# Four edits to one attention kernel's schedule: where head outputs are placed, when right operands are due, which masks TensorE adds, and how outputs reach x

## The chip, the cores and the metric

The kernel runs on one core of a Trainium2 chip. The metric is the device time of one execution, in microseconds; less is better. A core has TensorE (PE, matrix products, with weight loads shown as PEld), VectorE (DVE), ScalarE (ACT), GpSimd (POOL), and SyncE (SP), which here issues nearly all transfers between DRAM and on-chip memory. Each engine takes its instructions in the order in which the kernel was written down; an instruction that waits holds up everything behind it on its engine.

## The reference, cut

```python
batch, n_heads, seq, head_dim = 4, 8, 768, 64          # block = 32, 24 blocks
scores = (1/sqrt(64)) * q @ k.transpose(0, 1, 3, 2)
scores = where(mask, scores, -1e9)      # window, first/last rows and columns, 3 random blocks a row
attn = exp(scores - max); attn = attn / (attn.sum(-1) + 1e-09)
x = (attn @ v).transpose(0, 2, 1, 3).reshape(B, S, 512)
mixed = real(fft(fft(x, axis=1), axis=2))
u = x + mixed
un = (u - mean(u)) / sqrt(var(u) + 1e-06)              # over the 512 features
out = u + maximum(un @ w_ch1, 0) @ w_ch2               # 512 -> 2048 -> 512
```

## The kernel before

The kernel has two kinds of work: attention, which makes x, and the mixer (Fourier transform, normalizing, channel products), which makes the output from x. They overlap: while batch b is in attention, the mixer of batch b-1 runs beside it, and the mixer of the last batch ends the kernel.

**Attention** goes through 16 pairs n (4 batches with 4 pairs of heads each; batch b has pairs 4b to 4b+3). A pair has 12 units: two halves of the queries ("first" and "second", 384 each) by six key chunks of 128. Two units make a slot, so a pair has six slots. For a unit, TensorE computes scores s (`scores`, L578). The mask is applied in one of two ways. "By TensorE": four more short products (L588) per slot add a large negative number to the scores, and ScalarE's exponential (L598) writes e directly. Or by VectorE: the exponential (L606) stays in TensorE's accumulator, and a multiplication with a mask of 0 and 1 (L608) writes e. The first way is used for batch 0 and then as long as `masks["by_pe"]` is true; it also leaves an addition of e into `acc` per unit (L633 on VectorE or L638 on GpSimd). A slot's e goes to the product with v one or two slots later (`values`, o, L652).

A finished half of a pair, oT, must become columns of x. `place` does it by three transposes on TensorE (xt, L675) and a copy on ScalarE into x (L676). For the pairs 9, 10, 11, 13, 14 and 15 `place_blocks` (L691) does it by transfers: 16 for each half, each of a 32-row piece with 12 KB. There are two buffers of x for each half, so batch b uses those of batch b-2, and the copy of its first pair must wait until the stores of batch b-2 to the output (`out_dram<-x`, L1157) have landed.

**The mixer** of a batch goes: sums of the softmax turned and inverted (st L746, r L749), x scaled by them (`scale_x`, L761), the Fourier transform and the normalizing (utp transposes L992, un L951), and a turn of the normalized rows through DRAM: `un_blocks` writes `far` (L1011), `un_back` reads it as unT (L1020). `right` (L1052, VectorE) makes the four right operands of the Strassen products from unT. Then the channel products start: a `quad` of seven products (xp, yp, z, L1090, with the additions L1095 on VectorE), then `channels`: y (L1146), added to x by VectorE (L1149).

**What sets the order.** One function, `slot`, writes one slot of attention and what stands between it and the next. Channel steps wait in a list `late` and are dealt out at a pace. Mixer steps before the channels wait in `apart`; a planner (`gap`) puts each in when its own running estimate of each engine's time, `when`, says that the step's inputs are ready. Transposes and placements wait in `short` with an estimated ready time. `BACK` is how long after `un_back` the planner holds the right steps of kind "b" back; each of these steps has an estimated cost. `LEAVES` is how long after TensorE's estimated time a placement that reuses x of batch b-2 becomes ready. In `slot`, such a placement of the first half is queued at slot 5 of the batch's first pair, that of the second half at slot 1 of its second pair:

```python
if reuse:
    until(lambda: (b - 2, 0) in finished)
    at = when["PE"] + LEAVES
```

`begin` queues a batch's mixer, and with it a step `go`, which opens the channels and sets `masks["by_pe"]` to false.

Of the kernel before, what the change touches and what calls it, by code (L numbers as in the profile page):

```python
# [11 lines left out]
FP32 = mybir.dt.float32  # L12
# [10 lines left out]
def _words(ap, n):  # L23

    return bass.DRamTensorHandle(ap.tensor.name, (2 * n,), I32)
# [74 lines left out]
def kernel(  # L100
# [14 lines left out]
    nc = tc.nc  # L115
# [4 lines left out]
    P = 128  # L120
    C = S // P
    BLK = 32
# [7 lines left out]
    T = C // 2  # L130
# [54 lines left out]
    far_p = ctx.enter_context(tc.tile_pool(name="far_p", bufs=1, space=bass.MemoryType.DRAM))  # L185
# [7 lines left out]
    when = {"PE": 0.0, "ACT": 0.0, "DVE": 0.0, "POOL": 0.0}  # L193
    free = {"m": [0.0, 0.0], "t": [0.0]}

    def busy(engine, us, after=0.0):
        when[engine] = max(when[engine], after) + us
        return when[engine]

    def bank(tag):  # L200

        at = free[tag].index(min(free[tag]))
        when["PE"] = max(when["PE"], free[tag][at])
        free[tag][at] = float("inf")
        return tag, at

    def give(which, at):
        free[which[0]][which[1]] = at + HOP
# [91 lines left out]
    def bit(n):  # L300
# [5 lines left out]
                      in_=bass.AP(tensor=_words(sampled_blocks, NB * NR), offset=0,  # L306
                                  ap=[[0, NB], [1, 2 * NB * NR]]))
# [135 lines left out]
    for w, w_sb in ((w_ch1, w1_sb), (w_ch2, w2_sb)):  # L443
        rows, cols = w.shape
# [42 lines left out]
    by_pe, to_gather = set(), deque()  # L487
    masks = {"by_pe": True}

    turned, e_of, acc_of, o_of, sums_of, x_of, sp_of = {}, {}, {}, {}, {}, {}, {}  # L490
# [101 lines left out]
    def weigh(u, s):  # L592
        n, w = divmod(u, UP)
        half, c = divmod(w, C)
        e = ep.tile([P, 2, HS], FP32, tag="e", name="e")
        e_of[u] = e
        if u in by_pe:
            nc.scalar.activation(out=e, in_=s[:, :, 0:HS], func=ACT.Exp, scale=scale)  # L598
            e_at[u] = busy("ACT", 0.8, max(s_at[u], e_free.pop(u - 2 * SLOT, 0.0))) + HOP
            if n >= NP:  # L600
                to_gather.append(u)

            if w >= UP - SLOT:
                gather_to(u)
        else:
            nc.scalar.activation(out=s[:, :, 0:HS], in_=s[:, :, 0:HS], func=ACT.Exp, scale=scale)  # L606
            m = mask[:, c, half * HS:(half + 1) * HS].rearrange("p (o s) -> p o s", o=1)
            nc.vector.tensor_tensor(out=e, in0=s[:, :, 0:HS], in1=m.broadcast_to([P, 2, HS]),  # L608
                                    op=ALU.mult)
            e_at[u] = busy("DVE", 0.97, busy("ACT", 0.8, s_at[u]) + HOP) + HOP  # L610
            gather_to(u)
            if n >= NP:
                gather(u)

    def gather_to(u):
        while to_gather and to_gather[0] <= u:
            gather(to_gather.popleft())
# [49 lines left out]
    def place(n, half):  # L667

        b, j = pairs[n]
        oT = o_of.pop((n, half))  # L670
        if j == 0:
            x_of[b, half] = xp.tile([P, T, DM], FP32, tag=("xA", "xB")[half], name="x")
        xt, at = ps_t.tile([P, 512], FP32, tag="t", name="xt"), bank("t")
        for c in range(T):
            nc.tensor.transpose(xt[:, c * P:(c + 1) * P], oT[:, c * P:(c + 1) * P], ident)  # L675
        nc.scalar.copy(out=x_of[b, half][:, :, j * P:(j + 1) * P],  # L676
                       in_=xt[:, 0:HS].rearrange("p (c f) -> p c f", c=T))
        give(at, busy("ACT", 0.5, busy("PE", 0.45, oT_at[n, half]) + HOP))

    def in_blocks(n):  # L680

        return n > 2 * NP and n % NP > 0

    def place_blocks(n, half):
        b, j = pairs[n]
        oT = o_of.pop((n, half)).rearrange("p (c t d) -> p c t d", t=P // BLK, d=BLK)
        for g in range(P // BLK):
            for t in range(P // BLK):  # L690
                nc.sync.dma_start(  # L691
                    out=x_of[b, half][BLK * t:BLK * t + BLK, :, j * P + BLK * g:j * P + BLK * (g + 1)],
                    in_=oT[BLK * g:BLK * g + BLK, :, t, :])

    def into_sums(key, j, sp):
        if j == 0:
# [281 lines left out]
    def mixer(b, xA, xB):  # L978
# [34 lines left out]
        def un_back():  # L1013

            for half in range(2):
                unT[half] = tr_p.tile([P, ND, T * P], FP32, tag="tr", name="unT")
                of = lines[half].rearrange("m (g j) (k a i) -> a j k (m g) i",
                                           j=BLK, a=P // BLK, i=BLK)
                for a in range(P // BLK):
                    nc.sync.dma_start(  # L1020
                        out=unT[half][BLK * a:BLK * a + BLK].rearrange(
                            "j k (g i) -> j k g i", i=BLK),
                        in_=of[a])
            state["back"] = max(when["PE"], state["ready"]) + BACK[b > 0]

        t, s = {}, {}
        K1, K2 = slice(0, ND // 2), slice(ND // 2, ND)

        def spare_room():
            if s:  # L1030
                return
            rest, n, w = room(5, [P, ND * HS], "t4"), HS * ND // 2, P * ND // 2
            t[4] = rest[:, 0:n].rearrange("p (k n) -> p k n", n=HS)
            for i in (1, 3, 4):
                s[i] = rest[:, n:n + w].rearrange("p (k n) -> p k n", n=P)
                n += w

        def right(j, *tiles):

            spare_room()  # L1040
            if 1 not in t:
                both = room(4, [P, ND, HS], "t12")
                t[1], t[2], t[3] = both[:, K1, :], both[:, K2, :], unT[1][:, K1, :]
            b11, b21 = unT[0][:, K1, :], unT[0][:, K2, :]
            b12, b22 = unT[1][:, K1, :], unT[1][:, K2, :]

            def part(ap):
                return ap.rearrange("p k (t n) -> p k t n", n=P)[:, :, tiles[0]:tiles[-1] + 1, :]

            to, a, c = {1: (t[1], b12, b11), 2: (t[2], b22, t[1]), 3: (b12, b22, b12),  # L1050
                        4: (t[4], b21, t[2])}[j]
            tt(out=part(to), in0=part(a), in1=part(c), op=ALU.subtract)  # L1052
# [225 lines left out]
        if not last:  # L1278
            before = first + [pq[1], ar[0][1], ar[1][1], sp[0][1],
                              pq[2], wh[0][1], ft[0][1], ar[0][2], ar[1][2], sp[0][2],  # L1280
                              pq[0], wh[0][2], ft[0][2], ar[0][0], ar[1][0], sp[0][0],
                              sp[1][1], wh[0][0], ft[0][0], sp[1][2], wh[1][1], ft[1][1],
                              sp[1][0], wh[1][2], ft[1][2], wh[1][0], ft[1][0]]
            after = ([("-", un_back, 0.0, 0.0, 0.0)] + le +
                     [("b", lambda i=i: right(i, 0, 1, 2), 0.0, 0.0, 1.0) for i in (1, 2, 3, 4)])
        rest = []
        for r in range(2 if last else 0):
            rest += [(lambda p=p: quad(p), 7 * PRODUCT) for p in range(4 * r, 4 * r + 4)]
# [2 lines left out]
        for r in range(0 if last else NF // 4):  # L1291
# [9 lines left out]
    MOST, LEAST = 9.6, 2.5  # L1301
    COVER = 100.0
    AHEAD = 2.2
    BACK = 13.0, 12.0
    ALONE = 3.0
    LEAVES = 9.0
    SP = UP // SLOT
    SB = SP * NP
    W_PACE = 1.42
# [1 line left out]
    asked = set()  # L1311
    needed = set()
    state = {"paired": False, "total": None, "w": 0, "got": 0, "owed": 0.0, "ready": 0.0,
             "back": 0.0}

    def channel_step():
        late.popleft()[0]()

    def behind(kind):
# [64 lines left out]
    def begin(b):  # L1384


        before, after, rest = mixer(b, x_of[b, 0], x_of[b, 1])
        any_of = len(late) + len(apart) + 4 * len(rest)
        hold = 2 * T
        apart.extend((*step, any_of) for step in norm_steps(b) + before)  # L1390
        apart.extend((*step, hold) for step in after)

        def go():
            late.extend(rest)
            masks["by_pe"] = False
        apart.append(("-", go, 0.0, 0.0, 0.0, hold))

    def rest():
# [19 lines left out]
    def slot(sl):  # L1418
        phase, r = divmod(sl, SB)
        n, s = divmod(sl, SP)  # L1420
# [26 lines left out]
            keep_mask = mask_step(2 * (sl // 3 - 1) + sl % 3 // 2)  # L1447
        for u, ps in got:
            weigh(u, ps)
        if keep_mask:  # L1450
            keep_mask()
        if BY_VECTOR <= n + 1 < len(pairs):
# [16 lines left out]
        if s >= (5 if reuse else 3) and (n, 0) in oT_at and once(n):  # L1469
            b, j = pairs[n]  # L1470
            at = oT_at[n, 0]
            if reuse:
                until(lambda: (b - 2, 0) in finished)
                at = when["PE"] + LEAVES
            if in_blocks(n):
                place_blocks(n, 0)
            else:
                short.append(("t", at, lambda: place(n, 0)))
# [5 lines left out]
        if sl < B * SB and n % NP == 1 and s == 1:  # L1484
            b = pairs[n - 1][0]
            at = oT_at[n - 1, 1]
            if b >= 2:
                until(lambda: (b - 2, 1) in finished)
                at = when["PE"] + LEAVES
            short.append(("t", at, lambda: place(n - 1, 1)))  # L1490
# [43 lines left out]
        while short and (not more or soon) and (  # L1534
                s in must or len(short) > 1 or phase == 0 or soon or sl == B * SB):
            ready = [i for i in short if max(i[1], min(free[i[0]])) <= when["PE"] + 0.1]
# [149 lines left out]
```

## Time and profile before

| What | Value |
|---|---|
| Median of 3 runs | 1059.56 us (1056.76 to 1062.27) |
| Profiled execution | 1059.17 us; span 1057.5 us |
| Mean granted TensorE clock | 0.993 |
| TensorE busy | 1022.8 us (97%), 4338 products |
| VectorE, ScalarE, GpSimd busy | 675.3, 356.2, 240.2 us |
| Placements by transfer x<-oT | 192 of 12 KB, 585 to 1494 ns to issue, median 597 |
| Right steps L1052, first batch | 237.96 to 244.2 us |

Busy time is time in which an engine executed something. TensorE's idle time is 34.7 us in all: 9.6 us before 226, 10.5 after 942 (mostly the last stores), and the rest in short stretches at the hand-overs from one batch's transform to its channel products and to the next batch's attention. A line of the chain of waits gives start, length, engine, operation and line; a line of the wait list gives the engine, the line that waited, what for, the sum in us, how often, and the longest.

### The profile page before, as it was taken

The numbers are of one execution on the slowest core, as the hardware profiler recorded it, in microseconds if no ns is written. First come the engines' busy times: TensorE is split into PE (matmuls) and PEld (weight loads), VectorE is DVE, ScalarE is ACT, GpSimd is POOL, SyncE is SP. The second block draws the span as 40 slices with busy tenths as digits, with TensorE's granted clock in tenths as the row PEclk, the third lists the DMA queues.
The fourth block names the chain that finished last, engine by engine and source line by source line (L and its number), as shares of the span: only waits on it lengthen the run. The fifth ranks groups of instructions, "written<-read, shape, count | busy, mean of one in ns | idle before, by whom it ended". The sixth has DMA issues, their size and how long they took to land.

```text
span 1057.5 us, 12421 instructions
## 1 busy us (share of the span) xinstructions
PE 1022.8 (97%) x4338; PEld 530.7 (50%) x4338; DVE 675.3 (64%) x1235; ACT 356.2 (34%) x718; POOL 240.2 (23%) x270
## 2 busy tenths in 40 slices
PE   8989999997999999999999999899999999999996
PEld 4434345433465553444444654444444654578585
DVE  5899795968745744564578467565457364674663
ACT  6988755562020111342441212153220211210210
POOL 1000183565000100454553001256520001000000
PEclk9999999999999999999999999999999999999998
DMA  7757422292000124212230003821000001000001
GB/s 210 228 177 227 107 47 46 50 140 36 1 0 21 40 30 76 62 32 50 41 56 1 1 10 93 107 39 27 11 11 6 0 1 38 23 1 1 1 17 46
DMA packets 160385, 55.71 MB, mean 53 GB/s; under 512 B 145708, under 2 KB 151098, under 8 KB 160314
## 3 DMA queue, kind: packets, MB, share of 16 engines
q1 hardware_dynamic: 159062, 54.10, 23.9%
q10 hardware_dynamic: 1220, 0.72, 0.3%
q8 instruction: 36, 0.59, 0.2%
q14 instruction: 35, 0.29, 0.1%
q0 software_dynamic: 32, 0.01, 0.0%
HBM read 41.44 MB, written 11.01 MB: 50 GB/s over the span
## 4 chain that ended last, share of the span: by engine, by line
PE 82%; DVE 8%; ACT 3%; DMA 3%; issue 2%; SPq 1%; ACTq 0%; DVEq 0%
PE y L1146 23%; PE z L1090 15%; PE s L578 10%; PE o L652 9%; PE yp L1090 7%; PE yy L1211 7%; PE xp L1090 4%; PE zp L856 2%; ACT e L598 1%; DMA out_dram<-x 1%; PE sp L719 1%; PE s L588 1%; DVE t L1052 1%; DVE x L926 1%; DVE acc L633 1%
## 5 line engine op out<-in xcount | busy, mean ns | idle before, releaser
L638 POOL TENSOR_TENSOR acc<-acc,e 128x384 f32<-128x384 f32 x162 | 163.6, 1046 | 103.8 <-DVE e L608 84.5
L578 PE MATMUL s<-qT,kT 64*128 64x384 f32 x768 | 155.2, 518 | 13.0 <-DVE e L608 6.5
L652 PE MATMUL o<-e,vr 128*64 128x384 f32 x768 | 142.7, 499 | 0.0
L1146 PE MATMUL y<-w_sb,hB 128*128 128x512 f32 x288 | 129.2, 600 | 0.3 <-DVE x L1149 0.3
L1146 PE MATMUL y<-w_sb,hA 128*128 128x512 f32 x288 | 127.9, 595 | 0.0
L1149 DVE TENSOR_TENSOR x<-y,x 128x512 f32<-128x512 f32 x72 | 49.7, 691 | 119.9 <-PE y L1146 119.8
L608 DVE TENSOR_TENSOR e<-s,mask 128x768 f32<-128x768 f32 x90 | 82.0, 951 | 54.9 <-ACT s L606 47.6
L578 PEld LDWEIGHTS s<-qT,kT 64*128 64x128 f32 x768 | 63.8, 186 | 92.3 <-ACT e L598 25.2
L638 POOL TENSOR_TENSOR acc<-e 128x384 f32<-128x384 f32 x42 | 47.1, 1143 | 254.5 <-ACT e L598 124.6
L606 ACT ACTIVATE s<-s 128x768 f32<-128x768 f32 x90 | 68.4, 792 | 89.4 <-PE s L578 89.1
L1090 PE MATMUL z<-unT,t 128*128 128x384 f32 x256 | 93.1, 486 | 2.0 <-DVE hA L1095 2.0
L598 ACT ACTIVATE e<-s 128x768 f32<-128x768 f32 x102 | 77.7, 811 | 48.5 <-PE s L588 32.0
L1146 PEld LDWEIGHTS y<-w_sb,hB 128*128 128x128 f32 x288 | 53.9, 192 | 67.6 <-issue 65.8
L1146 PEld LDWEIGHTS y<-w_sb,hA 128*128 128x128 f32 x288 | 53.7, 190 | 63.7 <-issue 60.2
L652 PEld LDWEIGHTS o<-e,vr 128*64 128x64 f32 x768 | 48.2, 137 | 71.6 <-issue 68.7
L1095 DVE TENSOR_TENSOR hA<-z,hA 128x384 f32<-128x384 f32 x64 | 35.7, 558 | 69.8 <-PE z L1090 69.6
L1099 ACT ACTIVATE hA<-hA 128x384 f32<-128x384 f32 x64 | 33.5, 523 | 129.3 <-DVE hA L1095 129.3
L1090 PEld LDWEIGHTS z<-unT,t 128*128 128x128 f32 x256 | 48.6, 190 | 36.8 <-DVE hA L1095 3.1
L1099 ACT ACTIVATE hB<-hB 128x384 f32<-128x384 f32 x64 | 33.5, 523 | 86.6 <-DVE hB L1095 86.6
L1110 ACT COPY hA<-xp 128x384 f32<-128x384 f32 x32 | 15.3, 478 | 116.0 <-PE xp L1090 116.0
L1090 PE MATMUL z<-t,w_sb 128*128 128x384 f32 x128 | 46.9, 489 | 5.0 <-DVE e L608 3.4
L1090 PE MATMUL z<-t,t 128*128 128x384 f32 x128 | 47.8, 497 | 0.0
(208 smaller groups left out, 1367.0 us busy)
## 6 DMA issues: line engine op xcount, KB each, us to landing
wraw<-in_moe_w_ch_dram SPq DMA_DIRECT2D x32, 512.0 KB
vr<-in_v_dram SPq DMA_DIRECT2D x30, 192.0 KB
far<-un SPq DMA_DIRECT2D x18, 256.0 KB
unT<-far SPq DMA_DIRECT2D x24, 192.0 KB
qb<-in_q_dram SPq DMA_DIRECT2D x44, 96.0 KB
kb<-in_k_dram SPq DMA_DIRECT2D x44, 96.0 KB
x<-oT SPq DMA_DIRECT2D x192, 12.0 KB
out_dram<-x SPq DMA_DIRECT2D x11, 252.0 KB
```

The costliest lines, as they stand in the source:

```text
L578: nc.tensor.matmul(s[:, i, 0:HS], kT[rows, c * P:(c + 1) * P], qT[rows, queries], start=True, stop=u not in by_pe)
L598: nc.scalar.activation(out=e, in_=s[:, :, 0:HS], func=ACT.Exp, scale=scale)
L606: nc.scalar.activation(out=s[:, :, 0:HS], in_=s[:, :, 0:HS], func=ACT.Exp, scale=scale)
L608: nc.vector.tensor_tensor(out=e, in0=s[:, :, 0:HS], in1=m.broadcast_to([P, 2, HS]), op=ALU.mult)
L638: nc.gpsimd.tensor_add(out=acc[:, i, :], in0=start[:, i, :], in1=e[:, i, :])
L652: nc.tensor.matmul(o[D * i:D * i + D, :], vt[:, i, c, :], e[:, i, :], start=(c == 0), stop=(c == C - 1))
L1090: nc.tensor.matmul(to, a[:, k, :], c[:, k, :], start=(k == 0), stop=(k == ND // 2 - 1))
L1095: tt(out=to, in0=ps, in1=a, op=ALU.add)
L1099: nc.scalar.activation(out=h, in_=h, func=ACT.Relu)
L1146: nc.tensor.matmul(y, hs[0, half][:, l, m * P:(m + 1) * P], w2_sb[:, 4 * r + l, :], start=(l == 0), stop=(l == 3))
L1149: nc.vector.tensor_tensor(out=x[:, m, :], in0=y, in1=x[:, m, :], op=ALU.add)
L1211: nc.tensor.matmul(ps, a[:, k, :], c[k // 2][:, k % 2, :] if isinstance(c, list) else c[:, k, :], start=(k == 0), stop=(k == 3))
```

## The change

Four edits.

1. `place_blocks` writes oT to a DRAM buffer `row` in four transfers, then reads it into x in four; the second four wait for the first. It had 16 transfers within the chip.
2. `BACK` has a value for each batch; 13 and 12 stay for batches 0 and 1, and batch 2 has 15 instead of 12. The estimated cost of a right step in batch 0 goes from 1.0 to 1.7.
3. `masks["by_pe"]` becomes false with the first channel step that is written, not with `go`.
4. A first half that reuses x of batch b-2 is placed in the next slot right after that slot's exponentials are written, instead of waiting in `short`; for the second half `LEAVES` goes from 9 to 13.

```diff
     def place_blocks(n, half):
         b, j = pairs[n]
-        oT = o_of.pop((n, half)).rearrange("p (c t d) -> p c t d", t=P // BLK, d=BLK)
+        rows = far_p.tile([BLK, T, P // BLK, P], FP32, tag=f"oT{half}", name="row", bufs=2)
+        oT = o_of.pop((n, half))
         for g in range(P // BLK):
-            for t in range(P // BLK):
-                nc.sync.dma_start(
-                    out=x_of[b, half][BLK * t:BLK * t + BLK, :, j * P + BLK * g:j * P + BLK * (g + 1)],
-                    in_=oT[BLK * g:BLK * g + BLK, :, t, :])
+            nc.sync.dma_start(
+                out=rows.rearrange("r c t f -> r (c t) f")[:, :, BLK * g:BLK * g + BLK],
+                in_=oT[BLK * g:BLK * g + BLK, :].rearrange("r (ct d) -> r ct d", d=BLK))
+        for t in range(P // BLK):
+            nc.sync.dma_start(
+                out=x_of[b, half][BLK * t:BLK * t + BLK, :, j * P:(j + 1) * P],
+                in_=rows[:, :, t, :])
...
-            state["back"] = max(when["PE"], state["ready"]) + BACK[b > 0]
+            state["back"] = max(when["PE"], state["ready"]) + BACK[b]
...
-                     [("b", lambda i=i: right(i, 0, 1, 2), 0.0, 0.0, 1.0) for i in (1, 2, 3, 4)])
+                     [("b", lambda i=i: right(i, 0, 1, 2), 0.0, 0.0, 1.0 if b else 1.7)
+                      for i in (1, 2, 3, 4)])
...
-    BACK = 13.0, 12.0
+    BACK = 13.0, 12.0, 15.0
...
-    LEAVES = 9.0
+    LEAVES = 13.0
...
     def channel_step():
+        masks["by_pe"] = False
         late.popleft()[0]()
...
         def go():
             late.extend(rest)
-            masks["by_pe"] = False
...
         for u, ps in got:
             weigh(u, ps)
+        if state["place"]:
+            state["place"]()
+            state["place"] = None
...
             if reuse:
                 until(lambda: (b - 2, 0) in finished)
-                at = when["PE"] + LEAVES
-            if in_blocks(n):
+                state["place"] = lambda: place(n, 0)
+            elif in_blocks(n):
                 place_blocks(n, 0)
             else:
                 short.append(("t", at, lambda: place(n, 0)))
```

In the changed program VectorE has as many instructions as before, TensorE 12 more products with their weight loads, ScalarE 3 more and GpSimd 2 fewer instructions in the listing, and SyncE 96 fewer transfers. The order on each engine is the same up to about 235 us of the time before.

More of the change, by code (lines that the diff above doesn't have):

```diff
@@ L1313 @@
     state = {"paired": False, "total": None, "w": 0, "got": 0, "owed": 0.0, "ready": 0.0,
-             "back": 0.0}
+             "back": 0.0, "place": None}
     def channel_step():
+        masks["by_pe"] = False
         late.popleft()[0]()
```

## The prediction

> **What bounds the kernel now.** I read the first and fourth parts of the page, then the table of windows cut at the hand-overs between stages, then TensorE's waits, then the chain inside the bad windows. Page, busy time and chain:
>
> ```profile
> PE 1022.8 (97%) x4338; PEld 530.7 (50%) x4338; DVE 675.3 (64%) x1235; ACT 356.2 (34%) x718; POOL 240.2 (23%) x270
> ...
> PE 82%; DVE 8%; ACT 3%; DMA 3%; issue 2%; SPq 1%; ACTq 0%; DVEq 0%
> ```
>
> TensorE bounds, and no edit here takes work from it. So only its idle time (34.7 us) and the time in which it ran at a lower clock can be won. The windows say where that is (columns: window, length, busy time by engine with counts, PEclk granted, DMA share, GB/s):
>
> ```profile
> 238.00:247.00 9.00, 5.64 (x22) 3.02 (x19) 8.93 (x8) 1.53 (x3) 6.37 (x5) 0.98 0.69 104
> 247.00:260.00 13.00, 11.01 (x40) 4.55 (x38) 11.95 (x20) 4.07 (x7) 2.93 (x4) 0.89 0.00 0
> ...
> 400.00:425.00 25.00, 23.04 (x77) 9.45 (x76) 11.50 (x15) 4.68 (x8) 4.35 (x4) 0.93 0.41 66
> ...
> 655.00:695.00 40.00, 34.71 (x139) 15.56 (x139) 22.43 (x33) 12.09 (x25) 10.79 (x12) 0.96 0.74 109
> ...
> 895.00:942.00 47.00, 45.61 (x151) 26.96 (x150) 31.52 (x62) 12.42 (x24) 0.00 (x0) 1.00 0.06 17
> ```
>
> Idle: 3.36 + 1.99, then 1.96, 5.29 and 1.39 us, all at the hand-overs between batches. Between them TensorE is full (260 to 400 idles 0). TensorE's longest waits name the blockers:
>
> ```profile
> PE s L578 <- DVE e L608: 6.5, 3, 3.7
> ...
> PE z L1090 <- DVE e L608: 3.4, 1, 3.4
> PE z L1090 <- DVE hA L1095: 2.0, 1, 2.0
> PE z L1090 <- DVE t L1052: 1.6, 1, 1.6
> ```
>
> The chain in the window 385 to 440 explains the 1.96:
>
> ```profile
> 407.49 2.79 DMA out_dram<-x
> ...
> 410.51 0.48 ACT x L676
> 410.99 0.71 ACT s L606
> 411.72 0.97 DVE e L608
> 412.73 2.35 PE s L578 x8
> 415.08 4.71 PE y L1146 x8
> ```
>
> The copy that places a first half reuses an x buffer whose last store is still under way. It sits at ScalarE's head, and the next exponential queues behind it. The scores after it cost 2.35 instead of 1.49, eight y 4.71 instead of 3.43. The window 655 to 695 has the same with the second half:
>
> ```profile
> 679.45 7.46 DMA out_dram<-x
> ...
> 687.09 0.48 ACT x L676
> 687.57 0.71 ACT s L606
> 688.36 0.97 DVE e L608
> 689.37 2.50 PE s L578 x8
> ```
>
> **The sum's base.** The profiled execution took 1059.17 us (span 1057.5 and 1.7 around it); the median is 1059.56, so terms are taken from 1059.17. A measurement here tells some 0.5% from no change: faster means below 1054.3, slower above 1064.9.
>
> **Masks on TensorE until channels begin.** Three more slots are masked by L588 (0.33 us a slot, 1.0 in all) in place of multiplies L608 on VectorE (six of 0.95). Each now leaves an addition to VectorE L633 (1.0) or to GpSimd, so VectorE is little lighter. What changes is order: before, the first product (z L1090, 242.60 on) waits behind four right steps (237.96 to 244.2), two mask multiplies (244.27, 1.73), the reciprocal and five scalings L761 (246.40 to 250.82). After, the three slots' scores run while the right steps run, the scalings spread over the slots, and the first seven-product group starts with its operands ready. From 235.8 to 269.5 TensorE took 33.7 us for work that sums to 25.8 by its rows (s 1.49, o 1.44, quad 9.03, two of them, xp and yp 1.29 each, the sums): 5.35 idle, the rest low clock (0.63 granted in 247 to 251). After: 25.8 + 1.0 + a new wait. An exponential that writes e directly needs an e buffer, which GpSimd's additions (four units, done at 243.45) free; my replay of the rows puts that wait at 1.3. Sum 28.1 to 28.3: **−5.4**, ends −3 (GpSimd each time 1 us later, and the clock drop stays) and −6.5 (no wait). The 1.7 for the right steps (rows: 0.95 to 1.75) only shifts where the planner puts them, and is in this term.
>
> **First halves behind the next exponentials, batch 2.** After, the exponentials of the next slot stand before the copy L676 on ScalarE, with four more y ahead of it on TensorE. The copy is wanted at about 412.9; the store lands at 410.3. Behind the copy then waits nothing urgent. Gone: 1.96 idle, 0.86 on s, 1.36 on y: 4.2, and from the whole window (21.4 us for 17.1 of work) **−4.3**; ends −2 (idle gone, clock drop not) and −4.5.
>
> Here a page speaks to the size. The row: after 1.96 us of idle the granted clock was 0.50 for 414 to 416 and 0.69 for 416 to 418. The Trainium skill ("TensorE: Matmul & The Clock Gate", Part 1) has the clock halve after an idle window of about 3.4 us; by it the 1.96 would cost no clock and this term would be −2.0, but the trace disagrees, and the trace decides.
>
> **Batch 3: first half, second half (LEAVES 13), due time of the right steps (15).** Before, from 656.0 to 698.75: 42.7 us for 34.7 of work, so 8.0 lost: waits 1.58 and 3.71, s 2.50, o 2.37 for 1.44, and crumbs. After, all scores come ahead of the first product, so the right steps hold nobody (−1.6). But the second half's copy still needs the stores that land at 686.9. SyncE's order is unchanged: four kb loads took 6.6 us (670.41 to 677) behind the unT reads, then the six stores. The copy now stands behind two more exponentials, and the last two queue behind it. The work TensorE has without these two slots ends near 681.3; the first score it can then run comes at 689.3. That is 8.0 idle and about 2.0 of lower clock (as after the 3.71: 0.57 in 690 to 694), 10.0 lost: **+2.0**, ends +3.3 and −8.0 (the stores land before the copy is reached).
>
> **Outputs in eight transfers.** Twelve halves: 16 SyncE issues x<-oT at 0.597 (9.6 us) become four row<-oT, a wait for these to land, and four x<-row. Bounds of an issue: 0.6 (x<-oT, 12 KB) and 1.28 (unT<-far, 192 KB in 128-byte pieces); of a landing: 2.8 (410.3) and 7.5 (686.9). A half: from 4 × 0.6 + 2.8 + 4 × 0.6 = 7.6 to 4 × 1.28 + 7.5 + 4 × 0.6 = 15.0 instead of 9.6; I take 8, since DMA share here is near 0.1 as at 410. Behind SyncE's new wait queue the next pair's qb and kb loads, which are a pair ahead (kb lands near 458 or 496, used a stage later). The trace has one wait for these placements by others that matters: VectorE's scaling at 800.33 waited 3.10, and TensorE did not feel it. The last flip of an output comes some 9 us earlier (one quad less before it), which covers all up to 15: **0**.
>
> **The last hand-over.** With the placement moved, the channel steps left for 876 to 905 run out earlier: in the new order five utp transposes stand in a row where before each had y between. Replaying the rows: the y after the last product end at +14.2, the chain of utp, normalizing (GpSimd's 1.6 in it) and spreading at about 20.3; idle 3.9 instead of 1.2: **+2.5**, ends 0 and +4.
>
> Sum: −5.4 − 4.3 + 2.0 + 2.5 = −5.2: 1059.17 − 5.2 = **1054.0**.
>
> **Rivals.** (1) *Batch 3's stall goes too.* For it: the stores' own data is ready before SyncE gets to them; against: the SyncE order and the unT backlog are the same. Every microsecond of earlier landing gives one. All of it: −5.4 − 4.3 − 7 + 1.5 = −15.2: 1044. (2) *Slower: the DRAM hop sets the last transform.* At 733.12 to 799.06 SyncE carries 64 placements on end; the scaling at 800.33 follows the last, and behind it is the chain that the last hand-over exposes. If a landing of 128-byte pieces takes over 12 us, a half costs 5 + 12 + 2.4 + 12 = 31 on SyncE and in landing against 12; less the 9 of cover that is +10, and the sum is +5 or worse: 1064 to 1070. Against: DMA share is 0.09 in 695 to 830. A page speaks for it: the Trainium skill ("DMA: Bandwidth & Descriptors", Specifications) wants 512 bytes or more and has smaller writes read and rewritten; no row here shows 128-byte writes to DRAM. (3) *The masks' gain is eaten*: e buffers held by GpSimd stop TensorE for 5 us instead of 1.3, after which it resumes at a low clock: about 1058.5. (4) *Batch 3's copy waits longer*: each microsecond of landing after 687 costs one, with the last two exponentials behind it; from 697.5 the whole is slower than 1064.5: 1065. (5) *It does not do what it says*: that ScalarE still takes the copy first; the new order puts the exponentials ahead, so nothing is given to it.
>
> **Numbers.** Forecast 0.41 (its own range 1049 to 1059, half of it below 1054.3); rival 1: 0.25; 2: 0.11; 3: 0.13; 4: 0.10. Faster 0.20 + 0.25 = 0.45; same 0.21 + 0.13 = 0.34; slower 0.21. The range takes in rival 1 to its near side, and the edge of 2 and 4: 1044 to 1064.
>
> **What would show it.** Right: the 3.4 wait of z on e gone; idle in 400 to 425 near 0 and y at 3.43 for eight; one long wait of s near 681 to 689 with L676 waiting for out_dram; POOL or ScalarE named for a wait near 243; one utp wait of 2 to 4 us before 905. Wrong: no wait near 685 (rival 1), L761 waiting over 10 us for x<-row (2), a low clock after 245 (3).

## The result, and the profile after

The changed kernel took 1056.17 us (median of 20 runs, 1054.27 to 1059.40), the kernel before 1059.47 (20 runs, 1056.71 to 1062.27). The ratio is 0.9976, 95% interval 0.9966 to 0.9985: by it 2.5 us faster, clear of no change, and about half of the forecast 5.2 (the two medians differ by 3.3). The profiled execution took 1054.71 us (span 1052.8). It gained 4.5 on the one profiled before, so the pair of profiles shows more than the ratio; the rest of this document looks for the cause of both differences.

Lines in the changed kernel are shifted: z is L1094 (was L1090), y L1150 (L1146), the right steps L1056 (L1052), the stores L1161 (L1157).

The page of the changed kernel, busy time and the chain by engine:

```profile
PE 1023.6 (97%) x4350; PEld 531.4 (50%) x4350; DVE 672.1 (64%) x1232; ACT 356.4 (34%) x718; POOL 236.1 (22%) x264
...
PE 85%; DVE 5%; ACT 2%; SPq 2%; DMA 2%; issue 2%; POOL 1%; ACTq 0%; DVEq 0%; POOLq 0%
```

TensorE still bounds; VectorE's share of the chain fell from 8% to 5%. The same windows (busy time by engine, granted clock, DMA share, GB/s):

```profile
238.00:247.00 9.00, 7.08 (x42) 2.92 (x37) 8.79 (x7) 3.97 (x6) 5.79 (x4) 1.00 0.50 88
247.00:260.00 13.00, 13.00 (x44) 7.78 (x43) 7.49 (x16) 4.08 (x9) 3.86 (x4) 1.00 0.00 0
...
400.00:425.00 25.00, 25.00 (x90) 11.18 (x89) 12.68 (x17) 5.55 (x10) 5.76 (x6) 1.00 0.37 91
...
655.00:695.00 40.00, 35.02 (x137) 15.08 (x137) 24.83 (x31) 13.51 (x27) 21.40 (x20) 0.91 0.61 93
...
895.00:942.00 47.00, 46.43 (x156) 29.66 (x156) 33.31 (x66) 11.83 (x23) 0.52 (x1) 0.96 0.03 6
```

At the first hand-over (238 to 260) TensorE's idle time fell from 5.35 to 1.92 us and the granted clock is 1.00; 400 to 425 has no idle time left. Batch 3's hand-over is no better: about the same idle time (5.29 before, 4.98 after), at a granted clock of 0.91 instead of 0.96.

The 1.9 us that stay at the first hand-over are a wait of s for an exponential (L598), and the chain shows GpSimd's additions ahead of it:

```profile
238.74 5.06 POOL acc L638 x3
...
243.82 0.82 ACT e L598
...
244.69 0.92 PE s L578 x4
```

TensorE's waits in the changed kernel (sum, count, longest):

```profile
PE s L578 <- ACT e L598: 7.6, 11, 2.1
PE s L578 <- DVE e L608: 5.8, 3, 3.7
...
PE utp L996 <- DVE un L955: 1.3, 3, 0.7
PE utp L996 <- ACT unT L997: 0.7, 1, 0.7
```

The waits of z (3.4, 2.0 and 1.6) are gone. The mask multiply still stops s for 3.7, and utp now waits 2.0 in four pieces, all at the last hand-over. In the timeline of TensorE, batch 3's hand-over is (start, length, operation; idle time before it and what ended it):

```profile
674.01 2.93 PE L578 MATMUL s<-qT,kT 64*128 64x384 f32 x8 [3.67 <-DVE e L608]
676.88 2.83 PE L652 MATMUL o<-e,vr 128*64 128x384 f32 x8
681.01 1.78 PE L578 MATMUL s<-qT,kT 64*128 64x384 f32 x8 [1.31 <-DVE e L608]
```

The first wait isn't the copy's. VectorE's timeline shows whose it is:

```profile
666.90 1.18 DVE L1056 TENSOR_TENSOR t<-unT 128x768 f32<-128x768 f32 x1
668.11 1.64 DVE L1056 TENSOR_TENSOR t<-unT,t 128x768 f32<-128x768 f32 x1
669.67 1.75 DVE L1056 TENSOR_TENSOR unT<-unT 128x768 f32<-128x768 f32 x1
671.35 1.74 DVE L1056 TENSOR_TENSOR t<-unT,t 128x768 f32<-128x768 f32 x1
673.01 1.81 DVE L608 TENSOR_TENSOR e<-s,mask 128x768 f32<-128x768 f32 x2
```

Four right steps stand ahead of a slot's two mask multiplies, and with the slot's exponentials (ScalarE, 667.82 to 669.32) long done, TensorE waits for VectorE. The second wait is the copy's; the chain there:

```profile
671.12 7.42 DMA out_dram<-x
...
679.09 0.81 ACT s L606
...
680.00 0.97 DVE e L608
...
681.01 1.78 PE s L578 x8
```

The copy ends last. Without the first wait the scores and o behind it would run earlier, and the second wait would be longer by as much. So the 3.67 cost no time of their own as long as the copy keeps its place; this is worked out from the order, not run.

**A measure by stretch.** To compare kernels I took every product of TensorE in order, gave it a distance to the next product, one price for each line and shape from the trace before, and summed: that is "work". Elapsed time less work is "lost": idle time, low clock, and wider spacing of products. The level of a column depends on the prices; the differences down a column are what counts. Its growth over the same stretches of work, from each trace:

| us lost | first hand-over | to batch 2 | batch 2 | to batch 3 | batch 3 | to the last | last |
|---|---|---|---|---|---|---|---|
| before | 7.8 | 0.2 | 4.6 | 5.4 | 9.3 | 2.9 | 2.0 |
| changed, profile of 1054.71 | 2.5 | 0.8 | 0.4 | 6.3 | 10.1 | 3.3 | 4.3 |
| e5, changed, 1053.63 | 2.4 | 0.8 | 0.4 | 6.3 | 9.5 | 3.3 | 3.6 |
| e9, changed, 1056.83 | 1.8 | 0.8 | 0.4 | 6.3 | 11.7 | 3.3 | 3.6 |
| e10, changed, 1056.23 | 1.9 | 0.8 | 0.4 | 6.3 | 11.5 | 3.3 | 3.6 |
| e1, masks alone | 1.8 | 0.8 | 0.1 | 5.8 | 9.0 | 2.8 | 2.0 |
| e2, first half alone | 10.9 | 0.5 | 0.7 | 5.7 | 9.6 | 2.8 | 2.0 |
| e3, due times alone | 7.8 | 0.2 | 3.0 | 5.6 | 11.9 | 5.0 | 4.9 |
| e4, blocks alone | 6.9 | 0.2 | 3.0 | 5.4 | 9.1 | 2.8 | 2.0 |
| e6, both due times undone | 1.8 | 0.8 | 0.4 | 6.0 | 8.0 | 2.8 | 2.0 |
| e7, BACK undone | 1.8 | 0.8 | 0.4 | 6.3 | 3.8 | 2.8 | 2.0 |
| e8, second half later | 1.8 | 0.8 | 0.4 | 6.1 | 4.5 | 2.8 | 2.0 |
| e11, masks and LEAVES | 2.5 | 0.8 | 0.1 | 6.1 | 3.6 | 2.8 | 2.0 |
| e12, LEAVES undone | 1.8 | 0.8 | 0.4 | 6.0 | 11.9 | 3.3 | 3.6 |

The extra mask products add 0.7 to the work and are not in it. Where a stretch is cut moves some tenths between neighbours: with batch 2's taken to 425 us of the time before, the change gains 3.6 there instead of 4.2, and the stretches between lose about 1.1 more instead of 1.9.

Up to the first hand-over the order is the same everywhere, and yet the lost time differs between executions by up to 1.9, which the table leaves out. The same products start at these times in the profile of 1054.71 and in e9:

```profile
231.20 0.95 PE L737 MATMUL sp<-acc,pick 128*32 128x384 f32 x8
```

```profile
233.12 0.95 PE L737 MATMUL sp<-acc,pick 128*32 128x384 f32 x8
```

TensorE is idle 9.2 us up to there in the first and 10.1 in the second, and the mean granted clock is 1.000 and 0.993; what makes that is not traced.

### The profile page after: what moved, and what is told of

It reads as the page before. It is cut to its first block, busy times and chain, and to the rows that moved or that the text cites. A ratio compares the mean times of both kernels' runs of the same rounds, so it can differ in the third digit from the quotient of the medians.

```text
span 1052.8 us, 12348 instructions
## 1 busy us (share of the span) xinstructions
PE 1023.6 (97%) x4350; PEld 531.4 (50%) x4350; DVE 672.1 (64%) x1232; ACT 356.4 (34%) x718; POOL 236.1 (22%) x264
## 4 chain that ended last, share of the span: by engine, by line
PE 85%; DVE 5%; ACT 2%; SPq 2%; DMA 2%; issue 2%; POOL 1%; ACTq 0%; DVEq 0%; POOLq 0%
PE y L1150 23%; PE z L1094 16%; PE s L578 10%; PE o L652 9%; PE yp L1094 8%; PE yy L1215 7%; PE xp L1094 4%; PE zp L860 2%; PE s L588 1%; PE sp L723 1%; ACT e L598 1%; SPq L230 1%; DMA out_dram<-x 1%; POOL acc L638 1%; PE sp L737 1%
## 5 line engine op out<-in xcount | busy, mean ns | idle before, releaser
L1150 PE MATMUL y<-w_sb,hB 128*128 128x512 f32 x288 | 127.8, 595 | 0.0
L1150 PE MATMUL y<-w_sb,hA 128*128 128x512 f32 x288 | 127.7, 594 | 0.0
L608 DVE TENSOR_TENSOR e<-s,mask 128x768 f32<-128x768 f32 x84 | 76.3, 950 | 52.4 <-ACT s L606 47.4
L606 ACT ACTIVATE s<-s 128x768 f32<-128x768 f32 x84 | 63.6, 792 | 119.5 <-PE s L578 119.3
L598 ACT ACTIVATE e<-s 128x768 f32<-128x768 f32 x108 | 82.4, 811 | 53.7 <-PE s L588 34.5
L638 POOL TENSOR_TENSOR acc<-e 128x384 f32<-128x384 f32 x40 | 44.1, 1123 | 250.3 <-ACT e L598 124.1
L1094 PE MATMUL z<-unT,t 128*128 128x384 f32 x256 | 93.2, 487 | 0.0
L1150 PEld LDWEIGHTS y<-w_sb,hB 128*128 128x128 f32 x288 | 53.7, 190 | 66.3 <-issue 65.4
L1150 PEld LDWEIGHTS y<-w_sb,hA 128*128 128x128 f32 x288 | 53.9, 190 | 64.0 <-issue 60.4
L1103 ACT ACTIVATE hA<-hA 128x384 f32<-128x384 f32 x64 | 33.5, 523 | 119.9 <-DVE hA L1099 119.9
L1094 PEld LDWEIGHTS z<-unT,t 128*128 128x128 f32 x256 | 48.5, 190 | 34.4 <-DVE hA L1099 1.0
L1103 ACT ACTIVATE hB<-hB 128x384 f32<-128x384 f32 x64 | 33.5, 523 | 86.9 <-DVE hB L1099 86.9
L1114 ACT COPY hA<-xp 128x384 f32<-128x384 f32 x32 | 15.3, 477 | 116.6 <-PE xp L1094 116.6
L1094 PE MATMUL xp<-unT,w_sb 128*128 128x384 f32 x128 | 48.0, 498 | 0.0
L1094 PE MATMUL yp<-unT,w_sb 128*128 128x384 f32 x128 | 46.7, 487 | 0.4 <-DVE un L916 0.4
```

Source lines behind the costliest of these rows:

```text
L638: nc.gpsimd.tensor_add(out=acc[:, i, :], in0=start[:, i, :], in1=e[:, i, :])
L1094: nc.tensor.matmul(to, a[:, k, :], c[:, k, :], start=(k == 0), stop=(k == ND // 2 - 1))
L1103: nc.scalar.activation(out=h, in_=h, func=ACT.Relu)
L1150: nc.tensor.matmul(y, hs[0, half][:, l, m * P:(m + 1) * P], w2_sb[:, 4 * r + l, :], start=(l == 0), stop=(l == 3))
```

## The experiments: each part alone

All four start from the kernel before and share its runs (median 1058.86 of 23).

**e1, masks alone**, with the right steps' estimated cost:

```diff
     def channel_step():
+        masks["by_pe"] = False
...
         def go():
             late.extend(rest)
-            masks["by_pe"] = False
...
-                     [("b", lambda i=i: right(i, 0, 1, 2), 0.0, 0.0, 1.0) for i in (1, 2, 3, 4)])
+                     [("b", lambda i=i: right(i, 0, 1, 2), 0.0, 0.0, 1.0 if b else 1.7)
+                      for i in (1, 2, 3, 4)])
```

> The kernel before with the masks edit alone (and the right steps' estimated cost of 1.7 in batch 0). Theory A (the sum of the prediction, as the two profiles bear it out: first hand-over 5 us shorter): span 4 to 5.5 us under the kernel before, the 3.4 wait of z on e and the 2.0 on hA gone. Theory B (the profiled execution of the changed kernel was a lucky one, and the masks leave a wait on e buffers that differs between executions): 2 to 3 us under, with a wide spread of times.

Measured 1050.31 us, ratio 0.9909 (0.9893 to 0.9926): 8.5 by the medians, more than either theory gave, and more than twice the 3.3 of the whole change. In the table the first hand-over gives 6.0 of it and batch 2's gives 4.5. The latter nobody had asked for: in e1 the planner deals the channel steps differently, and 32 y in a row end ahead of batch 2's scores. The masks edit and the estimated cost of 1.7 were not run apart, so which of the two moves these steps is not shown. The chain of e1 there has no store in it:

```profile
392.46 13.73 PE y L1146 x32
406.19 0.33 PE xt L675 x3
406.52 1.49 PE s L578 x8
408.01 2.73 PE o L652 x16
410.74 1.49 PE s L578 x8
412.23 3.63 PE y L1146 x8
```

**e2, first half alone:**

```diff
         for u, ps in got:
             weigh(u, ps)
+        if state["place"]:
+            state["place"]()
+            state["place"] = None
...
-                at = when["PE"] + LEAVES
-            if in_blocks(n):
+                state["place"] = lambda: place(n, 0)
+            elif in_blocks(n):
```

> The kernel before with only the first half's placement moved behind the next exponentials, in batches 2 and 3. Theory A: the 1.96 us idle and the low clock at 412 to 420 go, 4 us under the kernel before; batch 3's stall of 3.7 on the second half stays as it is. Theory B (the stall moves to the second half's copy, in batch 2 too): 0 to 2 us under.

Measured 1056.28, ratio 0.9977 (0.9961 to 0.9993): 2.4 us, between the theories. In its profile batch 2's stall is gone (0.7 lost), batch 3's stays. So the edit does by itself what it says, and next to e1's edit, which empties the same stall, it has nothing left to win.

The profile of e2 shows something else too. Its twelve times lie in two groups, seven from 1053.2 to 1056.7 and five from 1058.9 to 1059.8, and the profiled execution (1059.53) is of the upper one. It loses 10.9 at the first hand-over, where before and e3 lose 7.8 and e4 6.9, with the same order on TensorE, VectorE, ScalarE and GpSimd. Timelines of TensorE, first before, then e2:

```profile
246.60 2.76 PE L1090 MATMUL z<-t,t 128*128 128x384 f32 x4
251.35 1.56 PE L1090 MATMUL z<-unT,t 128*128 128x384 f32 x4 [1.99 <-DVE hA L1095]
```

```profile
247.02 1.45 PE L1090 MATMUL z<-t,t 128*128 128x384 f32 x4
251.79 2.93 PE L1090 MATMUL z<-unT,t 128*128 128x384 f32 x4 [3.32 <-DVE hA L1095]
254.51 2.77 PE L1090 MATMUL yp<-t,w_sb 128*128 128x384 f32 x4
```

The granted clock from 246 to 250 is 0.57 in the first and 1.00 in the second, and from 252 to 258 it is 1.00 and 0.51. The wait ends at about the same time in both (251.35 and 251.79), since VectorE sets its end. So the low clock ahead of it cost no time of its own, and the one behind it cost about 3 us. What the masks edit takes away at this hand-over is therefore a range: from 6.9 to 10.9 was lost there without it, and 1.8 to 2.5 with it.

**e3, due times alone:**

```diff
-    BACK = 13.0, 12.0
+    BACK = 13.0, 12.0, 15.0
...
-    LEAVES = 9.0
+    LEAVES = 13.0
...
-            state["back"] = max(when["PE"], state["ready"]) + BACK[b > 0]
+            state["back"] = max(when["PE"], state["ready"]) + BACK[b]
```

> The kernel before with only BACK 15 for batch 2 and LEAVES 13. Theory A (the prediction's signs): batch 3's hand-over about even (0 to 2 us longer), the last hand-over 2.5 longer with five utp groups in a row: 2 to 4 us over the kernel before. Theory C (the due times win batch 3's stall, and the last hand-over costs nothing): 3 to 6 us under.

Measured 1066.55, ratio 1.0063 (1.0046 to 1.0080): 6.7 us by the ratio, slower than before, more than theory A's 2 to 4; theory C falls. Its profile loses 2.6 more in batch 3, 2.9 more at the last hand-over and 2.1 between.

Its profile also holds a check on a price of the prediction. The order up to batch 2's stall is that of before, and so is the wait. Timelines of TensorE, first before, then e3:

```profile
412.73 2.35 PE L578 MATMUL s<-qT,kT 64*128 64x384 f32 x8 [1.96 <-DVE e L608]
415.01 4.79 PE L1146 MATMUL y<-w_sb,hB 128*128 128x512 f32 x8
```

```profile
413.45 1.78 PE L578 MATMUL s<-qT,kT 64*128 64x384 f32 x8 [1.96 <-DVE e L608]
415.16 3.70 PE L1146 MATMUL y<-w_sb,hB 128*128 128x512 f32 x8
```

The granted clock in the window from 414 to 416 is 0.50 in the first and 1.00 in the second. The same idle time of 1.96 cost a drop of the clock in one execution and none in another (nor in e4, where it is 1.95): the stretch loses 4.6 in the one, 3.0 in the two others.

**e4, blocks alone:** `place_blocks` as in the change, nothing else.

```diff
     def place_blocks(n, half):
-        (16 transfers oT -> x)
+        rows = far_p.tile([BLK, T, P // BLK, P], FP32, tag=f"oT{half}", name="row", bufs=2)
+        (4 transfers oT -> rows, 4 transfers rows -> x)
```

> The kernel before with only the outputs placed through DRAM in eight transfers. Theory A (hidden): the same time within 1 us, and VectorE's wait of 3.1 at 797 stays or shrinks. Theory D (the hop costs something that the rows do not show, such as later k loads or stores, and eats part of the gain): 1 to 3 us over the kernel before.

Measured 1059.30, ratio 0.9994 (0.9983 to 1.0004). Theory A holds: VectorE no longer waits for a placement (3.10 us before). SyncE's timeline of e4 shows one half:

```profile
443.87 2.63 SPq L691 DMA_DIRECT2D row<-oT  x4
447.98 2.50 SPq L695 DMA_DIRECT2D x<-row  x4
```

From the last issue of row (446.50) to the first of x it is 1.5 us, so a half takes SyncE 6.6 us instead of 10.3 (445.35 to 455.67 in the trace before).

## The experiments: the changed kernel, and its due times

e5 to e8 share runs of the kernel before with median 1058.05 (17), e9 to e12 others with median 1058.85 (17).

**e5, the changed kernel again.**

> The changed kernel itself, once more. Its profiled execution took 1054.71 us, 1.5 under its median. Theory E (the masks and first-half terms hold, and the due times cost more in most executions than in the one profiled): a profile with a longer time loses more between 660 and 692, where TensorE waits 3.7 and 1.3 us and the clock decides; the first hand-over stays at 2.5 lost. Theory B (the masks' gain differs between executions): the first hand-over loses more than 2.5.

Measured 1056.30, ratio 0.9980 (0.9969 to 0.9990), as the first time. The profiled execution was again a short one (1053.63), so it decides nothing on the typical one.

**e6, both due times undone:**

```diff
-    BACK = 13.0, 12.0, 15.0
+    BACK = 13.0, 12.0, 12.0
...
-    LEAVES = 13.0
+    LEAVES = 9.0
```

> The changed kernel with BACK 12 for batch 2 and LEAVES 9 again. Theory E: the last hand-over's 2.3 us come back and batch 3's hand-over loses 9 instead of 10 to 12; 1049 to 1051 us, 5 to 7 under the changed kernel. Theory F (the due times need the other edits and pay with them, as the sum of the parts alone, -9.6 - 2.4 + 6.7, is not what the whole does): 1054 or more.

Measured 1051.36, ratio 0.9936 (0.9924 to 0.9949). This is theory E, just outside its ranges: 4.9 us under the changed kernel (e5), with 8.0 lost in batch 3 and the last hand-over back at 2.0.

**e7, BACK undone, LEAVES kept at 13:**

```diff
-    BACK = 13.0, 12.0, 15.0
+    BACK = 13.0, 12.0, 12.0
```

> The changed kernel with BACK 12 for batch 2, LEAVES stays at 13. If the right steps' due time alone is what costs: as the run with both undone, within 1.5 us (1048 to 1052). If LEAVES is what costs: near the changed kernel, 1055 to 1058.

Measured 1045.22, ratio 0.9885 (0.9869 to 0.9901), 11 us under the changed kernel (e5, by the medians) and 6 under e6: both expectations miss. The due time of the right steps costs everything, and LEAVES 13 is a gain of its own beside the old due time. Timeline of TensorE in e7, and below it that of ScalarE:

```profile
661.92 1.45 PE L1094 MATMUL xp<-unT,w_sb 128*128 128x384 f32 x4
...
665.98 1.53 PE L1094 MATMUL z<-t,w_sb 128*128 128x384 f32 x4 [1.31 <-DVE t L1056]
...
672.60 1.64 PE L578 MATMUL s<-qT,kT 64*128 64x384 f32 x8
674.16 2.80 PE L652 MATMUL o<-e,vr 128*64 128x384 f32 x16
676.89 1.56 PE L578 MATMUL s<-qT,kT 64*128 64x384 f32 x8
```

```profile
673.72 1.49 ACT L606 ACTIVATE s<-s 128x768 f32<-128x768 f32 x2
...
677.85 1.50 ACT L606 ACTIVATE s<-s 128x768 f32<-128x768 f32 x2 [1.26 <-PE s L578]
679.25 0.50 ACT L676 COPY x<-xt 128x384 f32<-128x384 f32 x1
```

With the old due time the group of seven products runs first (661.92 to 672.6), at the price of 1.31. What it asks of ScalarE (L1114 and L1103, done at 673.81) stands ahead of the copy. Then come the scores of two slots and their exponentials, and the copy behind them, at 679.25, waits for no store: they have landed under the group and these slots. With BACK 15 this group is behind all the scores that depend on the copy, and nothing covers the landing.

**e8, second half later**, BACK 12 and LEAVES 9:

```diff
-        if state["place"]:
-            state["place"]()
+        if state["place"] and sl >= state["place"][0]:
+            state["place"][1]()
             state["place"] = None
...
-                state["place"] = lambda: place(n, 0)
+                state["place"] = sl + 1, lambda: place(n, 0)
...
                 at = when["PE"] + LEAVES
-            short.append(("t", at, lambda: place(n - 1, 1)))
+            if b == B - 1:
+                state["place"] = sl + 3, lambda: place(n - 1, 1)
+            else:
+                short.append(("t", at, lambda: place(n - 1, 1)))
```

> The changed kernel with BACK 12 and LEAVES 9 as before, and batch 3's second half placed behind the exponentials of the slot three after the one that queues it, in place of by its due time. If the copy L676 in front of the exponentials is what stalls batch 3's hand-over: its 3.7 wait and the low clock behind it go, 5 to 6 us under the run with both due times undone, 1043 to 1046. If the stall goes on to the right steps or to a later slot: 1048 to 1051.

Measured 1046.05, ratio 0.9890 (0.9872 to 0.9907): 5.3 under e6, as the first expectation had it (its range ended at 1046). Its profile loses 4.5 in batch 3 instead of 8.0. The copy in front of the exponentials was the stall.

**e9 and e10, the changed kernel for its profile.** No edit; one time each, 1056.83 and 1056.23.

> The changed kernel once more, for its profile alone: its times run from 1053.6 to 1059.4, and both profiles so far lie in the lower part. If the clock at batch 3's hand-over makes the difference: a profile above 1056 loses more than 10.1 between the y before that hand-over and the second y after it, and the rest is as before, within 0.5 a stage. If it is the first hand-over: there.

> As the run before it: the changed kernel for its profile alone. A profile above 1056 with 12 or more lost at batch 3's hand-over speaks for the clock there; one with 4 or more at the first hand-over speaks for the masks.

Both lie near the median, and both lose 11.5 to 11.7 in batch 3 where the short executions lose 9.5 to 10.1; the first hand-over is not it. e10's 11.5 is just under the 12 that its expectation asked for, and two other stretches of e9 differ by 0.7 from the profile of 1054.71, both the other way, where 0.5 was allowed. Batch 3 is not the whole difference either: up to the first hand-over, e9 and e10 lose 1.4 to 1.9 more than the short executions. Timelines of TensorE, first e9, then e5, the shortest:

```profile
675.18 2.91 PE L578 MATMUL s<-qT,kT 64*128 64x384 f32 x8 [3.67 <-DVE e L608]
678.02 1.80 PE L652 MATMUL o<-e,vr 128*64 128x384 f32 x8
682.51 2.93 PE L578 MATMUL s<-qT,kT 64*128 64x384 f32 x8 [2.68 <-DVE e L608]
```

```profile
674.12 2.93 PE L578 MATMUL s<-qT,kT 64*128 64x384 f32 x8 [3.68 <-DVE e L608]
676.98 1.51 PE L652 MATMUL o<-e,vr 128*64 128x384 f32 x8
680.48 1.78 PE L578 MATMUL s<-qT,kT 64*128 64x384 f32 x8 [1.99 <-DVE e L608]
```

In these executions it is the clock behind the second wait that counts. In the profile of 1054.71 it stayed low after the first wait (o took 2.83), but that work stands in front of a wait whose end the copy sets, so it cost nothing there; the second wait was 1.31, and s behind it took 1.78. In e5 the clock came back sooner (o 1.51), the second wait was 1.99, and s behind it took 1.78 as well. In e9 the clock came back (o 1.80), the second wait was 2.68, and the clock dropped once more behind it (s 2.93), where every part of it counts. In e10 it dropped behind a second wait of 1.82, shorter than e5's (0.50 granted from 684 to 686). So neither the length of the wait nor an early return of the clock decides it. Over 20 runs of the changed kernel, time and mean granted clock go together (correlation -0.75, worked out from the runs' lists).

**e11, masks and LEAVES 13, nothing else:** e1's edit, and `LEAVES = 13.0`.

> The kernel before with the masks edit and LEAVES 13: neither the first half's placement nor the DRAM hop nor BACK 15. If LEAVES pays because the second half's copy then stands behind two exponentials when the stores land: as the best so far, 1044 to 1047. If it needs the first half's new place as well: 1048 to 1051, as the masks alone (1050.3).

Measured 1045.27, ratio 0.9878 (0.9860 to 0.9897; kernel before 1058.85 in 17 runs). Two of the edits, with the cost of 1.7 that goes with the first, give all that e7 has.

**e12, the changed kernel with `LEAVES = 9.0`**, BACK 15 kept.

> The changed kernel with LEAVES 9: BACK 15 stays. In batch 3 the order is that of the changed kernel, since the second half is placed at the same spot either way. If BACK 15 alone costs what the changed kernel loses to the run without it (1045.2): 1055.5 to 1058. If LEAVES matters beside it: 1059 or more, as LEAVES won 6 us without BACK 15.

Measured 1056.31, ratio 0.9975 (0.9964 to 0.9987): the changed kernel's time. With BACK 15 the value of LEAVES does nothing in batch 3, since a later rule of `slot` places the waiting half at slot 3 either way; apart from 12 products and 8 instructions of ScalarE at batch 2's hand-over, the traces of e12 and of the changed kernel have the same order. So the two due times belong together: at LEAVES 9, BACK 15 costs 4 to 5 us (e6 to e12, by the ratios and by the medians), and at LEAVES 13 it costs 10 to 11 (e7 to e5), because it also takes away what LEAVES wins.

## Why the prediction was half right

- **Masks: right.** The forecast was -5.4 with 1.0 of mask products in it. The profiles lose 5.3 less, up to 6.0 in e9, and the mask products cost 0.7, so -4.6 to -5.3 against the profile before. The wait on an e buffer was 1.93, and 1.2 in e1 and e9 (1.3 predicted), held by GpSimd as said. The closeness is in part luck: without the edit the same hand-over lost 6.9 in e4 and 10.9 in e2.
- **First half: the mechanism right, the size not.** -4.3 was 4.2 in the profiled pair, but e3 and e4 show the old stall at 3.0: 2.6 of gain. The first failed step is the 1.36 for slow y and most of the 0.86 for s: a clock drop in one execution, taken as the price of every one. The end I had given for it (-2) was closer. The Trainium skill ("TensorE: Matmul & The Clock Gate", Part 1) has the clock halve after an idle window of about 3.4 us. The trace before went against it (1.96 us, then 0.50); after the same 1.96 us, e3's clock stayed at 1.00, as that page would have it. And the credit belongs to e1's edit as much as to this one: e1 has the gain without the move.
- **Batch 3: what ends last right, the wait in front of it wrong.** 10.0 lost was forecast for after, and the profile has 10.1; +2.0 came as +0.8 there, because this measure gives 9.3 before where I had counted 8.0, and as +2.2 to +2.4 in e9 and e10. The copy's stores end the stall, as forecast. But "the right steps hold nobody" failed: in place of one wait of 8.0 there are two, and the first, of 3.7, is the mask multiply behind four right steps. The forecast asked which products wait for these steps and not what stands behind them in VectorE's queue. It also took both due times as one term. They pull apart: BACK 15 costs 11 us in this kernel (e7), and LEAVES 13 wins 6 where BACK stays at 12 (e6 to e7).
- **Last hand-over: the size right, the make-up not.** +2.5 forecast; +2.3 in the profile, +1.6 in e5, e9, e10 and e12. It was to be idle time, 3.9 instead of 1.2. The five utp groups do stand in a row, but they wait 2.0 in all, and the rest of the 2.3 goes with a lower granted clock, 0.76 from 893 to 897 and 0.82 from 897 to 901. e3 and e12 have it and e6, e7, e8 do not, so it comes from BACK.
- **Blocks: right.** 0; a landing of 1.5 lies below the lower bound of 2.8. Rival 2 falls: it needed a landing of over 12. The Trainium skill ("DMA: Bandwidth & Descriptors", Specifications) has transfers under 512 bytes read and rewritten; with 128-byte pieces written to DRAM no such cost is visible here (e4's time is the same).
- **The term that was missing.** This is the second failed step: "Between them TensorE is full" was read from before and carried over at no cost. The three stretches between hand-overs lost 8.5 before and 10.4 after: +1.9. Idle time is 0.4 of it (1.1 in 262 to 385, 425 to 655 and 700 to 876 before, 1.5 in the same work after, at a granted clock of 1.00 in both), such as yp's 0.18 on un behind a group of pq that had y beside it before. The rest is wider spacing in the new order, or belongs to batch 2's row by another cut (-3.6 there and +1.1 here); it is not traced to single products.

Against the profile before, the sum is: masks -4.6 to -5.3, batch 2 -2.6 to -4.2, batch 3 +2.2, the last +1.6, between +1.9; in all -1.5 to -3.8. The measured 2.5 (1.6 to 3.6 by the interval) lies in it. The forecast's 5.2 lacks the 1.9 and up to 1.7 of the clock. As the first hand-over of the kernel before is itself a range of 4 us, that the sum fits does not prove each term.

## What to carry to other kernels

When a copy must wait for a store, cover the landing with work whose share of the copy's engine stands ahead of the copy, and let the urgent instructions of that engine stand ahead of it too; delaying that cover (BACK 15) undid a gain of about four times what the change brought. Try due times one by one: of two numbers in one edit, one took away what the other wins, and the kernel with that one undone is 1.15% faster than before instead of 0.24%. A price that rests on a clock drop after a short idle time is a range, until a second execution shows the same drop.

## What the runs showed of the hardware

The same 1.96 us of idle TensorE was followed by a granted clock of 0.50 in one execution and 1.00 in another, and in one kernel 1.82 us by 0.50 (e10) and 1.99 us by 1.00 (e5). In these traces a low clock in front of a wait whose end another engine or a store sets cost no time of its own, and one behind it did: at the first hand-over, with one order, 0.57 ahead of the wait lost 7.8 us in all (before), and 0.51 behind it 10.9 (e2). Four DRAM writes of 48 KB in 128-byte pieces let a dependent read start 1.5 us after the last was issued (e4).
